# Two-layer decode with all gradients: gradient units taken out of the first attention's dp step, rows of g prepared one chunk sooner, two small output stores moved later

## Chip, cores and metric

The kernel runs on one core of one Trainium2 chip. The metric is the device time of one execution in microseconds (us), as the median of several runs. A core has TensorE (PE), which multiplies matrices into PSUM, VectorE (DVE), ScalarE (ACT) and GpSimd (POOL) for everything else, and SyncE (SP), which here only issues transfers. Transfers are also issued from the queues of ACT and POOL. All of them run on the same 16 DMA engines.

## The reference, cut to what matters

One token passes through attention A, a dense layer B, attention A again and B again. The same weights are used in both rounds. The output and the gradients of all inputs for a given `grad_out` are wanted.

```python
def _A_ref(x, k_cache, v_cache, wq, wo):            # Hq 32, Dh 128, Hkv 4, D 1024
    W = min(4096, max(256, Sk // 4))                # Sk 32768, so W = 4096
    q = (x @ wq) ...                                # one query row for each head
    k = jnp.repeat(k_cache[:, :, Sk - W:, :], rep, axis=1)
    v = jnp.repeat(v_cache[:, :, Sk - W:, :], rep, axis=1)
    p = _softmax(jnp.einsum("bhqd,bhkd->bhqk", q, k) * (Dh ** -0.5), axis=-1)
    return jnp.einsum("bhqk,bhkd->bhqd", p, v) ... @ wo

def _B_ref(x, w1, b1, w2):                          # F 3584
    h = jnp.einsum("bsd,df->bsf", x, w1) + b1
    act = h * jnp.tanh(softplus(h))
    return jnp.einsum("bsf,fd->bsd", act, w2)

x = A_x
x = x + _A_ref(_layernorm(x, axis=-1), A_k_cache, A_v_cache, A_wq, A_wo)
x = x + _B_ref(_layernorm(x, axis=-1), B_w1, B_b1, B_w2)
x = x + _A_ref(_layernorm(x, axis=-1), A_k_cache, A_v_cache, A_wq, A_wo)
x = x + _B_ref(_layernorm(x, axis=-1), B_w1, B_b1, B_w2)

_out, _vjp = jax.vjp(_f, A_x, A_k_cache, A_v_cache, A_wq, A_wo, B_w1, B_b1, B_w2)
_grads = _vjp(grad_out)
```

With one token, each weight is read for matrix-vector products, and each weight's gradient is a sum of two outer products, one for each round. The gradients of wq and wo are 8.4 MB each, those of w1 and w2 7.3 MB each. The gradients of the two caches are mostly zeros: 32768 rows for each of 4 heads, of which only the last 4096 take part.

## The kernel before

**Order.** The program is written by hand in the order in which each engine is to run it, and each engine works off its own queue in that order. It goes forward through A, B, A, B, then back: B of the second round (`dn_b1`), attention of the second round (`attn_bwd(1, ...)`), B of the first round, attention of the first round (`attn_bwd(0, ...)`), and a last stage that computes and stores the weights' gradients.

**Loads.** Weights come in chunks of 1 MB through a ring of eight slots (`ring`), which SP's queue fills in a planned order. The last loads are the eight chunks of wo for the first attention's backward (three of them in borrowed slots, which the program calls `lent`) and four chunks of wq; four more chunks of wq are still there from before.

**Zeros.** The zeros of the caches' gradients are 56 stores of 1 MB from the tile `zt`, issued by POOL (`zeros`, L265). The call can name a small tile, and POOL then first copies one element of it to `pz` (L260), so that the stores go out only when that tile is computed. In this way the zeros are spread over the run.

**First attention, backward** (`attn_bwd`, with l = 0). It goes in these steps; a hook is called in each, and the hooks of the first attention are `do1`, `dp1`, `dq1`, `dn1` and `units_a0`.
- *do*: eight chunks c of wo. Blocks are transposed on PE (L474), copied from PSUM to SBUF by ACT or DVE (`evac`, L306 and L309) and multiplied with the column of g (L493); some rows go to DVE (`rowdot`, L451). After each chunk comes `do1(c)`.
- *dp*: 128 small matmuls against V (L922) into two PSUM banks. For each bank DVE subtracts and multiplies, and the result goes to `DSX` (L928, L929). Then comes `dp1`.
- *dq*: 128 small matmuls of K with DSX (L938), then `DQC` (L940), its broadcast (L333) and `dq1`.
- *dn*: eight chunks t of wq, transposed and multiplied as in *do*. After each comes `dn1(t)`. The end is the layer norm's backward, with `units_a0` called twice inside, and the result is g0.

**Rows for the outer products.** A gradient unit (`unit_dw`, L1051) multiplies two rows of one operand with two rows of the other, one row for each round, so it wants these operands as rows on two partitions. They stand in `ROWS`, in four pairs of partitions that begin at 0, 32, 64 and 96. `rowize` transposes a set of columns on PE (L1010), lets ACT copy it to `rt` (L1013), and SP sends it into ROWS with two small DMAs (L1015). `rowize_f` does this with f's gradient through the tile `rf` (L857, L859, L861). `take_back` fetches rows that were put in DRAM earlier (L819). `twins` copies all pairs to a second set, `TWIN` (L1043), which units two blocks wide need. `store_rows` and `store_f` send the small outputs: `store_f` transposes b1's gradient `db` (L868), ACT copies it to the same `rf` (L870) and issues the store (L871); `store_rows` does so with `x4`, the output of the network, and with g0 (L321, L325, L326).

**Units.** `todo` holds four generators, one for each weight gradient. `work(n)` takes n steps from them in turn. A step makes 512 columns (PE, then `evac`) or, in the last stage, 1024; full stage tiles are stored by SP (L1025, or L1030 for a first half). `work` is called in `dp1` (four steps), in `units_a0` (twice four) and, until all is done, in the last stage. The stage tiles are K's and V's tiles as they come free, the ring's slots and the borrowed slots.

In *do*, chunk 5 has the hook that stores x4 and db, issues two zero stores and takes back four sets of rows; chunk 6 has `rowize` of `GA` and `GB` and `rowize_f`.

Of the kernel before, what the change touches and what calls it, by code (L numbers as in the profile page):

```python
# [23 lines left out]
TD = D // P  # L24
# [69 lines left out]
def kernel(  # L94
# [108 lines left out]
    GA = sb([P, TD, 2], BF16, "GA")  # L203
    GB = sb([P, TD, 2], BF16, "GB")
# [113 lines left out]
    def store_rows(col_bf, n, out_flat):  # L318

        b = big().bitcast(BF16)  # L320
        nc.tensor.transpose(b[0:n, 0:P], col_bf, ident_bf[:])  # L321
        k = so_n[0]
        so_n[0] += 1
        r = rt[0:n, 2 + k, :]
        nc.scalar.copy(r, b[0:n, 0:P])  # L325
        nc.scalar.dma_start(out_flat.rearrange("(t p) -> t p", p=P), r)  # L326
# [537 lines left out]
    def store_f(col):  # L864

        b = big().bitcast(BF16)
        for k in range(4):
            nc.tensor.transpose(b[0:7, k * P:(k + 1) * P], col[:].rearrange("p (c k) -> p k c", k=4)[:, k], ident_bf[:])  # L868
        r = rf[:, 0:512]
        nc.scalar.copy(r.rearrange("c (p k) -> c p k", k=4), b[0:7, 0:512].rearrange("c (k p) -> c p k", k=4))  # L870
        nc.scalar.dma_start(out_7.rearrange("(c j) -> c j", j=512), r)  # L871
# [135 lines left out]
    def rowize(cols, n, base, off):  # L1007

        b = big().bitcast(BF16)
        nc.tensor.transpose(b[0:2 * n, 0:P], cols[:].rearrange("p n l -> p (n l)"), ident_bf[:])  # L1010
        k = rt_n[0]
        rt_n[0] += 1
        nc.scalar.copy(rt[0:2 * n, k, :], b[0:2 * n, 0:P])  # L1013
        for l in range(2):
            nc.sync.dma_start(ROWS[base + l:base + l + 1, off:off + n * P].rearrange("o (t p) -> o t p", p=P),  # L1015
                              rt[l:2 * n:2, k, :])
# [96 lines left out]
    def work(n):  # L1113
        while n > 0 and any(todo):
            q = todo[turn[0] % 4]
            turn[0] += 1
            while q:
                try:
                    next(q[0])
                    n -= 1  # L1120
                    break
                except StopIteration:
                    q.popleft()
# [27 lines left out]
    x4 = sb([P, TD], BF16, "x4")  # L1151
    db = sb([P, TF], BF16, "db")
# [7 lines left out]
    def do1(c):  # L1160
        if c == 4:
            y = to_eight(YR, RT.rearrange("p a t s -> p (a t s)")[:, 0:512].bitcast(FP32))
            nc.vector.tensor_tensor(out=x4[:], in0=y, in1=x3[:], op=ALU.add)
        if c == 5:
            store_rows(x4[:], TD, out_0[0, 0, :])
            store_f(db)
            zeros(2, do1_acc[:, 4 * c:4 * c + 1])
        if c == 6:
            rowize(GA, TD, 32, 0)
            rowize(GB, TD, 96, 0)  # L1170
            rowize_f()
        if c == 5:
            take_back("AC", 96, NOFF)
            take_back("OC", 32, NOFF)
            take_back("NB", 64, 0)
            take_back("NA", 0, 0)

    def dp1():
        zeros(4)
        stage_free.extendleft(VS[:, g].rearrange("p t d -> p (t d)") for g in range(G))  # L1180
        work(4)

    def dq1():
        stage_free.extendleft(KT[:, g].rearrange("p t d -> p (t d)") for g in range(G))
# [4 lines left out]
    def dn1(t):  # L1189
        if t in (3, 6, 7):  # L1190
            zeros(2 if t == 3 else 1, dnp[:, t:t + 1])
        if t == 4:
            twins()
        if t == 5:
            todo[0].append(units_cols(0, 8, out_4))
# [8 lines left out]
    zeros(2, g0)  # L1204
    g0b = sb([P, TD], BF16, "g0b")
    nc.vector.tensor_copy(g0b[:], g0[:])
    store_rows(g0b[:], TD, out_1[0, 0, :])
    stage_free.extendleft(ring_t[:, i, :] for i in range(8))
    stage_free.extendleft(lent)
# [44 lines left out]
```

## Time and profile before

| | us |
|---|---|
| median of three runs | 458.82 (457.58 to 458.83) |
| profiled execution | 457.36 |
| its span, first to last instruction | 455.6 |
| PE busy | 317.9 (70%) |
| DVE busy | 261.9 (57%) |
| ACT busy | 210.6 (46%) |
| POOL busy | 38.9 (9%) |
| moved by DMA | 181.40 MB, mean 398 GB/s |

The span is that of one profiled execution; the execution's own time is 1.76 us longer. Busy shares are averages over stages with different limits. The windows of the profile list, for a stretch of the span, the busy time of each engine with the number of its instructions, then PE's granted clock, the busy share of the 16 DMA engines and their rate. The order of time lists start, length, engine, line, operation and shape; in brackets stands how long the engine was idle before, and what ended that. "SPq" and "POOLq" are the instructions of those engines that issue a transfer; when a transfer has landed is seen from who waited for it. The stages that the change touches are these: *do* of the first attention until 309.2 us, dp from 309.81, dq from 324.20, dn from 329.69, and the last stage from 349.48.

### The profile page before, as it was taken

What the parts mean: (1) busy time and instruction counts of PE and PEld (TensorE: products, weight loads), DVE (VectorE), ACT (ScalarE), POOL (GpSimd) and SP (SyncE); (2) the same over time, 40 slices, a digit from 0 to 9 for tenths busy, and PEclk for the clock granted to TensorE, in tenths of its full rate; (3) what the DMA queues carried; (4) which work ended last, traced back from release to release, by engine and by line L of the source; (5) the groups of instructions that cost most, each with busy time, mean ns of one, the idle gap of its engine ahead of it and who ended that gap; (6) DMA issues with size and microseconds to landing.
All of it is one profiled execution on the core that took longest, in us unless ns stands there. A gap on an engine that the chain in (4) does not pass through costs nothing. (4 is left out here: it accounts for less than half of the span.)

```text
span 455.6 us, 12833 instructions
## 1 busy us (share of the span) xinstructions
PE 317.9 (70%) x5681; PEld 244.5 (54%) x5681; DVE 261.9 (57%) x516; ACT 210.6 (46%) x244; POOL 38.9 (9%) x86
## 2 busy tenths in 40 slices
PE   3836443456798798986888577964696898789900
PEld 3835443445675698976887455954492122134500
DVE  4504737278532663763367558743176999988900
ACT  2501001011157675860373450750166999998900
POOL 1000000002032212102100001012112000000000
PEclk9955555565559897986698857995586555555555
DMA  8999999989999999999999999998399999999998
GB/s 335 419 423 420 416 420 420 418 316 422 391 426 420 423 421 414 400 420 422 425 416 423 424 393 365 422 418 359 129 368 404 412 410 420 415 422 419 404 409 324
DMA packets 28086, 181.40 MB, mean 398 GB/s; under 512 B 3675, under 2 KB 3703, under 8 KB 9591
## 3 DMA queue, kind: packets, MB, share of 16 engines
q1 hardware_dynamic: 19874, 121.84, 65.4%
q0 software_dynamic: 8064, 58.72, 31.3%
q8 instruction: 44, 0.72, 0.6%
q14 instruction: 12, 0.09, 0.0%
q10 hardware_dynamic: 92, 0.02, 0.0%
HBM read 81.84 MB, written 98.62 MB: 396 GB/s over the span
## 5 line engine op out<-in xcount | busy, mean ns | idle before, releaser
L309 ACT COPY ring<-BIG 128x1024 bf16<-128x1024 bf16 x51 | 50.6, 1013 | 49.7 <-PE BIG L474 44.5
L474 PE MATMUL BIG<-ident_bf,ring 128*128 128x128 bf16 x664 | 56.3, 242 | 4.4 <-ACT W L859 3.6
L474 PEld LDWEIGHTS <-ring 128*128 128x128 bf16 x768 | 54.6, 111 | 5.6 <-issue 5.1
L1051 PE MATMUL wide<-W 2*128 2x512 bf16 x228 | 50.3, 598 | 9.5 <-DVE KT L306 1.7
L451 DVE CUSTOM_DVE_ANT_0 junk<-ring,SC 128x1024 bf16<-128x1024 bf16 x32 | 38.9, 1215 | 9.2 <-DMA ring<-in_B_w_dram 8.8
L1051 PEld LDWEIGHTS <-W 2*128 2x128 bf16 x240 | 12.3, 102 | 53.6 <-issue 52.4
L493 PEld LDWEIGHTS <-ring 128*128 128x128 bf16 x864 | 30.1, 98 | 12.4 <-issue 6.1
L306 DVE COPY ring<-BIG 128x1024 bf16<-128x1024 bf16 x32 | 21.7, 689 | 25.1 <-PE BIG L474 14.0
L309 ACT CAST ring<-wide 128x1024 bf16<-128x1024 f32 (+1 forms) x36 | 33.8, 1028 | 2.3 <-PE wide L1051 1.3
L306 DVE CAST ring<-wide 128x1024 bf16<-128x1024 f32 (+1 forms) x28 | 32.6, 1199 | 3.1 <-PE wide L1102 1.0
L265 POOL DMA_DIRECT2D out_dram<-zt x56 | 29.7, 534 | 39.7 <-DMA out_dram<-zt 38.6
L309 ACT COPY KT<-BIG 128x1024 bf16<-128x1024 bf16 x22 | 21.7, 1008 | 22.4 <-PE BIG L652 20.5
L451 DVE CUSTOM_DVE_ANT_0 junk<-ring,DSX 128x1024 bf16<-128x1024 bf16 x24 | 29.4, 1224 | 0.8
L536 PE MATMUL MV<-NA,ring 128*128 128x1 bf16 x512 | 15.2, 165 | 13.0 <-DMA ring<-in_A_wq_dram 11.7
L474 PE MATMUL BIG<-ident_bf,W 128*128 128x128 bf16 x288 | 23.5, 228 | 0.4 <-issue 0.3
L309 ACT COPY W<-BIG 128x1024 bf16<-128x1024 bf16 x21 | 20.7, 1014 | 6.4 <-PE BIG L474 5.8
L306 DVE CAST KT<-wide 128x1024 bf16<-128x1024 f32 (+1 forms) x17 | 20.1, 1188 | 3.8 <-PE wide L1051 2.8
L536 PEld LDWEIGHTS <-ring 128*128 128x128 bf16 x512 | 14.6, 103 | 13.9 <-DMA ring<-in_A_wq_dram 12.4
L1102 PE MATMUL wide<-W 32*128 32x256 bf16 x128 | 21.0, 402 | 0.9 <-ACT ring L309 0.5
L309 ACT CAST VS<-wide 128x1024 bf16<-128x1024 f32 (+1 forms) x20 | 19.4, 1010 | 1.1 <-PE wide L1051 0.6
L474 PEld LDWEIGHTS <-W 128*128 128x128 bf16 x288 | 18.5, 112 | 0.7 <-issue 0.4
L347 PE MATMUL YR<-ring,AC 128*32 128x256 bf16 x208 | 10.3, 352 | 10.4 <-DMA ring<-in_B_w_dram 8.0
(272 smaller groups left out, 525.0 us busy)
## 6 DMA issues: line engine op xcount, KB each, us to landing
out_dram<-zt POOLq DMA_DIRECT2D x56, 1024.0 KB, 19.6
ring<-in_A_wq_dram SPq DMA_DIRECT2D x24, 1024.0 KB
ring<-in_A_wo_dram SPq DMA_DIRECT2D x14, 1024.0 KB
ring<-in_B_w_dram SPq DMA_DIRECT2D x13, 1024.0 KB
W<-in_A_wo_dram SPq DMA_DIRECT2D x10, 1024.0 KB
out_dram<-ring SPq DMA_DIRECT2D x8, 1024.0 KB
W<-in_B_w_dram SPq DMA_DIRECT2D x8, 896.0 KB
out_dram<-ring SPq DMA_DIRECT2D x11, 512.0 KB
```

The lines of the kernel that those rows point to most:

```text
L265: nc.gpsimd.dma_start(dst, zt[:])
L306: nc.vector.tensor_copy(dst, src)
L309: nc.scalar.copy(dst, src)
L347: nc.tensor.matmul(bank[32 * j:32 * j + 32, 0:n].rearrange("p (g a) -> p g a", a=m.shape[-1]), lhsT=vec.to_broadcast([P, 32]), rhs=m, star ...
L451: nc.vector.tensor_tensor_reduce(out=out, in0=a, in1=vec, scale=1.0, scalar=acc if i else 0.0, op0=ALU.mult, op1=ALU.add, accum_out=acc)
L474: nc.tensor.transpose(b[:, i * P:(i + 1) * P], block(w, i) if block else w[:, i * P:(i + 1) * P], ident_bf[:])
L493: nc.tensor.matmul(out, lhsT=w[:, i * P:(i + 1) * P], rhs=rhs_of(i), start=fresh[0], stop=last and i == n - 1, skip_group_check=True)
L536: nc.tensor.matmul(q_ps[:, h:h + 1], lhsT=ch[:, h * P:(h + 1) * P], rhs=NA[:, t, l:l + 1], start=(k == 0 and h == 0), stop=(k == TD - 1), ...
L1051: nc.tensor.matmul(b[:, 512 * i:512 * i + 512], lhsT=R[at:at + 2, lo:lo + P], rhs=R[at:at + 2, ro + 512 * i:ro + 512 * i + 512], start=Tru ...
L1102: nc.tensor.matmul(b[:, k * 256:(k + 1) * 256], lhsT=RT[32 * g:32 * g + 32, a, tp, :], rhs=YS[32 * g:32 * g + 32, :], start=True, stop=Tru ...
```

## The change

- `dp1` calls `work(4)` no more. The four units stay in `todo`.
- `rowize(GA)` and `rowize(GB)` come after chunk 5 instead of chunk 6. `rowize_f` stays after chunk 6.
- The four `take_back` calls come after chunk 6, behind `rowize_f`, instead of after chunk 5. On SP's queue the order is now GA and GB (four DMAs), f (two), AC, OC, NB, NA; it was AC, OC, NB, NA, GA and GB, f.
- `store_f(db)` moves from chunk 5 of *do* to chunk t = 1 of *dn*.
- `store_rows(x4)` moves from chunk 5 to the end of the attention's backward, ahead of `store_rows(g0b)`.

PE, DVE, POOL and SP have as many instructions as before. ACT has two fewer (243 for 245), because the four units that are left to the last stage are evacuated as two wide ones there.

```diff
@@ do1(c) @@
         if c == 5:
-            store_rows(x4[:], TD, out_0[0, 0, :])
-            store_f(db)
+            rowize(GA, TD, 32, 0)
+            rowize(GB, TD, 96, 0)
             zeros(2, do1_acc[:, 4 * c:4 * c + 1])
         if c == 6:
-            rowize(GA, TD, 32, 0)
-            rowize(GB, TD, 96, 0)
             rowize_f()
-        if c == 5:
             take_back("AC", 96, NOFF)
             take_back("OC", 32, NOFF)
             take_back("NB", 64, 0)
             take_back("NA", 0, 0)
@@ dp1() @@
         zeros(4)
         stage_free.extendleft(VS[:, g].rearrange("p t d -> p (t d)") for g in range(G))
-        work(4)
@@ dn1(t) @@
         if t in (3, 6, 7):
             zeros(2 if t == 3 else 1, dnp[:, t:t + 1])
+        if t == 1:
+            store_f(db)
         if t == 4:
             twins()
@@ after attn_bwd(0, ...) @@
     nc.vector.tensor_copy(g0b[:], g0[:])
+    store_rows(x4[:], TD, out_0[0, 0, :])
     store_rows(g0b[:], TD, out_1[0, 0, :])
```

## The prediction, made before the changed kernel ran

> **What bounds the kernel now.** I read the slices of the span first, then the windows of the last quarter, then the instructions in order of time around the one weak slice.
>
> ```profile
> DMA  8999999989999999999999999998399999999998
> GB/s 335 419 423 420 416 420 420 418 316 422 391 426 420 423 421 414 400 420 422 425 416 423 424 393 365 422 418 359 129 368 404 412 410 420 415 422 419 404 409 324
> ```
>
> A slice is 11.39 us. The DMA engines are full nearly everywhere; the slice at 319 to 330 moves 129 GB/s instead of some 415. The busy time by stretch says the same, finer:
>
> ```profile
> 305.00:350.00 45.00, 30.29 (x646) 25.10 (x646) 19.40 (x44) 15.25 (x22) 8.46 (x20) 0.63 0.78 314
> 308.00:310.00 2.00, 1.04 (x27) 0.90 (x28) 0.93 (x6) 0.00 (x0) 0.18 (x1) 0.50 0.76 303
> 310.00:312.00 2.00, 2.00 (x66) 2.00 (x64) 0.00 (x0) 0.00 (x0) 1.98 (x5) 0.50 0.59 230
> 320.00:322.00 2.00, 0.00 (x0) 0.00 (x0) 0.00 (x0) 0.00 (x0) 0.00 (x0) 0.50 0.72 293
> 322.00:324.00 2.00, 1.32 (x4) 0.16 (x4) 0.69 (x1) 0.95 (x2) 0.00 (x0) 0.50 0.05 20
> 326.00:328.00 2.00, 1.78 (x67) 1.69 (x64) 0.19 (x2) 0.00 (x0) 0.00 (x0) 0.50 0.00 0
> 328.00:330.00 2.00, 1.58 (x13) 1.30 (x14) 0.01 (x2) 0.26 (x1) 1.87 (x5) 0.50 0.34 131
> 340.00:342.00 2.00, 1.87 (x66) 1.68 (x62) 1.97 (x4) 0.30 (x1) 0.98 (x2) 1.00 0.72 270
> 350.00:433.00 83.00, 72.65 (x392) 25.79 (x384) 76.01 (x70) 78.95 (x86) 0.00 (x0) 0.50 1.01 414
> 433.80:452.00 18.20, 0.00 (x0) 0.00 (x0) 0.00 (x0) 0.00 (x0) 0.00 (x0) 0.50 1.02 408
> ```
>
> The last two columns are the DMA share and GB/s, the busy times before them PE, weight loads, VectorE (DVE), ScalarE (ACT), GpSimd (POOL). In the last row every engine is done and the DMA alone works for 18 us: the end is a queue of stores running dry, and the chain of waits, which calls ACT the bound up to 420 us, misses that. From 350 to 452 the share is 1.01 to 1.02 throughout. So the end falls earlier by just that DMA time which is idle before 350 and gets filled. Why it is idle stands in the order of time (column 1 start, column 2 length, in brackets the idle time before):
>
> ```profile
> 305.14 1.00 ACT L859 COPY W<-BIG 7x1024 bf16<-7x1024 bf16 x1 [4.05 <-DMA out_dram<-W]
> 306.20 0.81 PE L474 MATMUL BIG<-ident_bf,ring 128*128 128x128 bf16 x8 [3.57 <-ACT W L859]
> 310.06 2.10 POOL L265 DMA_DIRECT2D out_dram<-zt  x4
> 314.79 2.69 SPq L861 DMA_DIRECT2D W<-W  x2
> 322.43 1.01 PE L1051 MATMUL BIG<-W 2*128 2x512 bf16 x3 [8.55 <-DMA W<-W]
> 324.20 3.58 PE L938 MATMUL MV<-DSX,KT 128*128 128x8 bf16 x128
> 328.31 2.10 POOL L265 DMA_DIRECT2D out_dram<-zt  x4
> ```
>
> The four units of dp1 (L1051) wait at the head of PE's queue for rows of f that SP sent only at 314.79 to 317.48, and the dq matmuls (L938), which need none of them, stand behind. The next zero stores are tied to DQC, so the DMA engines run dry at 322. Earlier, rowize_f's copy (L859) waits for the store of b1's gradient to have left the shared row rf, PE waits for its bank, and the four zero stores of dp1 come late, at 310.06.
>
> **Change, part by part.**
> 1. *The store of db leaves c==5.* L859 waits for no store any more. PE's stall of 3.57 us goes; the ring copy that PE wanted next has its data (rowdot on that chunk ran at 300.47). dp1's zeros go from 310.06 to 306.5.
> 2. *No units in dp1.* The wait of 8.55 us and the units' own PE time (322.43 to 324.20, 1.77 us) go. With DSX's first half ready at 313.91 - 3.57 = 310.3 and its second at 311.8, the 3.58 us of dq run from 310.3 to 313.9, against 327.78: 3.57 + 8.55 + 1.77 = 13.9 us sooner. All that follows PE up to the last stage moves with it: the DQC zeros to 314.4, those at t = 3, 6, 7 (339.93, 344.60, 345.86) to 326.0, 330.7, 332.0, those on g0 (347.97) to 334.1, the first output store (351.16) to 337.3.
> 3. *The four units come back later:* units_a0 still makes eight, so four 512-column units are left to the last stage, where two are one evacuation of 1.01 us (ACT) or 1.22 us (DVE): about 1.1 us with the two engines side by side. The 18 us in which the DMA alone works cover it; without that cover it would cost 1.1.
> 4. *SP's order:* GA and GB rows (four DMAs) first, then f (two), then the four take-backs; ten small DMAs as before, behind the same loads. Six such issues took 10.58 us in a full queue (306.90 to 317.48), 1.76 each; ten from 297.3 end by 315. The DQC rows, ready at 329.67 - 13.9 = 315.8, are then not held. If the last six go out only from 311, when the loads are in, they end at 321.6: 6 us late for the twins, which the first wide stage unit (349.48 - 13.9 = 335.6) wants; in this trace the twins are issued by 337.78, 11.7 before it. I take nothing; the cover is the zeros, below.
> 5. *store_f in dn1 at t=1:* four transposes (0.38), a copy of 0.57 and an issue of 0.29 on ACT between ring copies with 0.6 to 0.7 us of idle each: nothing on the DMA's account. It waits for rowize_f's two DMAs to have read rf. Wanted at about 335.5 - 13.9 = 321.6; behind it on ACT stand all ring copies, for which PE waits. f's rows go out about 308 and, by the 5 us from 317.48 to 322.43, are in at 313. Nothing, with 8 us of room; the wait is rival four.
> 6. *x4's store before g0b's:* one transpose (0.22), one copy (0.26), one ACT issue (0.30), while PE and ACT wait for g0 anyway (1.32 us before L321): nothing; 0.8 at most.
>
> **Is the DMA then never dry?** One zero store is 1.05 MB, 2.56 us at 410 GB/s. From 306.5 to 323 the trace moved 338 GB/s x 16.5 us = 5.6 MB, all that was queued, dp1's four included; at 410 that lasts from 306.5 to 320.1. DQC's four (4.2 MB) come at 314.4 and last to 330.3; two at 326.0 to 335.4; two at 330.7 and 332.0 to 340.6; two at 334.1 to 345.7; outputs from 337.3. The margins are 5.7, 4.3, 4.7 and 8.4 us.
>
> **The sum.** Between 305 and 350 a share of 0.78 stands where 1.01 is full: 45 x (1.01 - 0.78)/1.01 = 10.2 us. By bytes: 314 x 45 = 14.1 MB takes 34.2 us at 414 GB/s (10.8 gained) or 35.3 at 400, about what zeros reached from 342 to 350 (9.7 gained). I take 10.2. Against it: the take-backs and rows that partly ran in a dip now run in full time. The take-backs are 38 KB in rows of 256 B, 152 of them; the small stores of the ACT queue between 296 and 332 used 0.1% of 16 engines' 36 us for 30 packets, 19 ns each, so 152 cost 2.9 us of one engine: 0.2 us if spread over 16, 2.9 if one engine carries all and everything ends with it. I take 0.4, near the spread end, since part ran under load before as well. Net 9.8: the span goes from 455.6 to 445.8, that execution from 457.36 to 447.6. The median of the runs shown, 458.82, lies 1.46 above the profiled execution; taken from it, **449.0**, which I forecast.
>
> **Rivals.**
> *Two engines carry the rows.* Each take-back ends on two partitions, so its rows may use two DMA engines, which then trail the rest by 2.9/2 = 1.45 us to the end. For it: 452 to 454 us shows a share of 0.62, so some engines do end later than others. Against: big stores follow on all engines and can only be late at the very end. Gain 10.2 - 1.45 = 8.75: 450.1. The Trainium skill (DMA: Bandwidth & Descriptors, "Why a DMA increments its semaphore by 16 and not by 1") says that a DMA runs on the largest number of engines up to 16 that divides the slowest dimension of both sides, which is two here; the trace does not name engines.
>
> *The first dip stays.* If ACT's copies, not the store's wait, pace the last wo chunk, dp starts no earlier and 2 x (1.01 - 0.76)/1.01 + 2 x (1.01 - 0.59)/1.01 = 1.3 us at 308 to 312 stay. dq is still 10.3 sooner, in time for the second dip. 458.82 - 8.5 = 450.3. For it: ACT has two ring copies (1.90 us) behind L859. Against: PE's stall names L859.
>
> *The dip moves.* The rows land late (point 4, behind zeros that now fill the DMA), and units_a0 (344.25 - 13.9 = 330.4) or the first wide stage waits. Outputs late by L leave a hole of L - 8.4. At L = 13, 4.6 us: 453.6. For it: 5 us from issue to use under load. Against: the rows are issued 15 us before their use. The Trainium skill (same page, "Queues, rings and completion order") says that an engine takes turns between queues by packets, so small rows would pass a long queue of zeros; the 5 us, under four queued zero stores (10 us of work), agree.
>
> *Slower: store_f holds ACT.* If f's rows are read late, ACT stops at t = 1, PE runs out of banks, and the zeros at t = 3 come late; beyond 4.3 us of hold the DMA runs dry, and beyond 4.3 + 9.8 = 14.1 us the kernel is slower than before, as when f is read at 336 instead of 313. At 16 us: 460.7. For it: this very row cost ACT 4.05 us in the other direction. Against: SP sends f sixth at the latest, and even sent from 311 on it is read at 326.6, a hold of 5 us that costs 0.7.
>
> *It does nothing:* if the end were set by engines (ACT 78.95 of 83 us busy), filling the DMA would bring nothing; but the engines, too, start 13.9 sooner, and they stop 18 us before the end. 458.8.
>
> **Chances.** Forecast 0.60 (449.0, its own range 447.4 to 450.0), two engines 0.12 (450.1), first dip stays 0.13 (450.3), dip moves 0.08 (451 to 456), does nothing 0.03, slower 0.04. The low end takes 10.8 by bytes and the spread of the runs (the lowest is 1.2 under the median): 446.7. The high end, 452.6, takes in the two middle rivals and the small part of the moved dip. What this measurement can tell from no change is about 0.3%, 1.4 us: faster 0.93, within it 0.03, slower 0.04.
>
> **What would show it.** Right: no ACT wait at L859; no L1051 between L922 and L938; dq over by about 314; the DQC zeros at 314 to 315; DMA share 1.0 in every slice from 305 on; the last unit some 10 to 14 us sooner than 433.76, the DMA alone for 15 us or more behind it. Wrong: a stretch under 0.9 between 320 and 350; ACT waiting at L870 for a DMA; PE waiting at L1051 for W<-W in units_a0 or the first wide units; last stores on a few engines only.

## The result, and the profile after

| | before | after |
|---|---|---|
| median (us) | 458.67 (457.58 to 458.83) | 450.82 (450.36 to 451.38) |
| ratio, 95% interval | | 0.9834 [0.9815, 0.9854] |
| span of the profiled execution (us) | 455.6 | 448.6 |
| last unit evacuated (us) | 433.76 | 423.05 |
| DMA mean (GB/s) | 398 | 404 |

The kernel is 7.85 us faster by the medians and 7.0 us by the two spans; the prediction said 9.8. The weak slice is gone, and a new weakness stands at the very end. These are the slices of the span after the change (11.2 us each; first row the DMA share in tenths, second what was moved):

```profile
DMA  8999999979999999999999999999999999999993
GB/s 336 420 420 418 421 420 418 418 312 427 393 421 422 422 420 415 398 420 423 424 423 422 427 423 419 424 393 422 424 406 415 400 417 419 417 421 408 377 408 143
```

The slice of 129 GB/s has become one of some 400. The last slice, 324 before, is 143 now. The windows of the kernel after say both more finely; the last two columns are DMA share and GB/s, the ones before them busy times of PE, weight loads, DVE, ACT and POOL and PE's clock:

```profile
305.00:350.00 45.00, 35.78 (x615) 24.27 (x613) 26.47 (x45) 22.81 (x31) 7.49 (x18) 0.62 1.01 416
308.00:310.00 2.00, 0.85 (x27) 0.78 (x27) 1.41 (x3) 0.00 (x0) 0.00 (x0) 0.50 1.00 415
...
322.00:324.00 2.00, 2.00 (x57) 2.00 (x54) 1.35 (x4) 1.75 (x2) 0.00 (x0) 1.00 1.04 436
...
326.00:328.00 2.00, 1.50 (x54) 1.44 (x55) 1.97 (x4) 0.01 (x1) 0.45 (x1) 1.00 1.02 395
...
430.00:440.00 10.00, 0.00 (x0) 0.00 (x0) 0.00 (x0) 0.00 (x0) 0.00 (x0) 0.50 1.02 407
440.00:444.00 4.00, 0.00 (x0) 0.00 (x0) 0.00 (x0) 0.00 (x0) 0.00 (x0) 0.50 0.28 114
444.00:446.00 2.00, 0.00 (x0) 0.00 (x0) 0.00 (x0) 0.00 (x0) 0.00 (x0) 0.50 0.06 27
446.00:448.60 2.60, 0.00 (x0) 0.00 (x0) 0.00 (x0) 0.00 (x0) 0.00 (x0) 0.50 0.03 13
```

Between 305 and 350 the share went from 0.78 to 1.01; both dips, at 308 and at 322 to 330, are filled. But from about 441 on almost nothing moves, and the span still lasts until 448.6. A share of 0.06 is one sixteenth: one DMA engine of 16 works, at 27 GB/s, which is a sixteenth of the 407 to 415 that all move together. Fifteen engines are out of work some 7 us before the end, and one is not; its last packet starts at 447.28. (The 1.3 us after that move nothing; the kernel before has 1.2 us of this kind.) Before the change the last stretch was far shorter: share 1.02 until 452, 0.62 in the next 2 us, 0.02 in the last 1.6.

The order of time after the change, for the places at which the prediction looked (start, length, engine, line, operation; in brackets the idle time before and what ended it):

```profile
299.38 1.00 ACT L859 COPY W<-BIG 7x1024 bf16<-7x1024 bf16 x1
...
304.24 2.10 POOL L265 DMA_DIRECT2D out_dram<-zt  x4
...
309.80 3.05 PE L938 MATMUL MV<-DSX,KT 128*128 128x8 bf16 x109 [1.08 <-issue]
...
313.38 2.10 POOL L265 DMA_DIRECT2D out_dram<-zt  x4
...
321.26 0.57 ACT L870 COPY W<-SC 7x512 bf16<-7x512 bf16 x1 [0.18 <-PE SC L868]
...
328.03 4.98 SPq L1043 DMA_DIRECT2D W<-W  x4
...
338.63 1.04 PE L1051 MATMUL wide<-W 2*128 2x512 bf16 x7 [1.72 <-DMA W<-W]
```

rowize_f's copy (L859) has no wait in brackets any more. dp's four zero stores leave at 304.24 instead of 310.06. No unit stands between dp and dq; the dq matmuls are over at 312.85 instead of 327.78, and DQC's zeros leave at 313.38 instead of 328.31. The last line is a wait that was not there before: the first wide units waited 1.72 us for the twins, whose four DMAs SP issued from 328.03 to 333.01.

**Where the time went, by idle DMA time.** Because the bytes are the same (181.40 MB), the span is the time in which the DMA is full plus the time in which it is not. I count the idle time of a stretch as its length times (1.01 - share)/1.01. From 305 to 360 (share 0.83 before, 1.01 after) it was 55 x 0.18/1.01 = 9.8 us and is 0. In the last stretch it was (2 x 0.39 + 1.6 x 0.99)/1.01 = 2.3 us and is (4 x 0.73 + 2 x 0.95 + 2.6 x 0.98)/1.01 = 7.3 us. So 9.8 us were gained and 5.0 us given back, together 4.8 of the 7.0. Most of the rest lies before the change acts: from 260 to 305 the profiled execution of before moved 399 GB/s and that of after 415, 0.72 MB or 1.7 us. That is not the change's doing: a kernel in which nothing ahead of 305 is altered (the first experiment) has 415 there as well, and the profiled executions of all twelve experiments have 407 to 422. A dip of 0.8 us at 419 to 423 in the changed kernel (share 0.70 and 0.90) is not in this sum.

### The profile page after: what moved, and what is told of

Its sections match the earlier page's. It is cut to its first block, busy times and chain, and to the rows that moved or that the text cites. A ratio compares the mean times of both kernels' runs of the same rounds, so it can differ in the third digit from the quotient of the medians.

```text
span 448.6 us, 12825 instructions
## 1 busy us (share of the span) xinstructions
PE 313.9 (70%) x5681; PEld 239.7 (53%) x5681; DVE 261.2 (58%) x516; ACT 210.0 (47%) x242; POOL 38.9 (9%) x86
## 2 busy tenths in 40 slices
DMA packets 28085, 181.40 MB, mean 404 GB/s; under 512 B 3674, under 2 KB 3702, under 8 KB 9590
## 4 chain that ended last, share of the span: by engine, by line
DMA 53%; PE 22%; ACT 7%; DVE 7%; issue 4%; SPq 1%; ACTq 0%; DVEq 0%
DMA ring<-in_B_w_dram 13%; DMA W<-in_A_wo_dram 8%; PE BIG L474 8%; DMA ring<-in_A_wq_dram 7%; DMA ring<-in_A_wo_dram 5%; DMA W<-in_A_wq_dram 5%; ACT ring L309 4%; DMA out_dram<-W 4%; DMA W<-in_B_w_dram 4%; PE TP L493 3%; DMA W<-dr_AC 2%; DMA W<-in_A_k_cache_dram 2%; PE wide L1051 2%; DVE KT L306 2%; PE SC L347 2%
## 5 line engine op out<-in xcount | busy, mean ns | idle before, releaser
L309 ACT COPY ring<-BIG 128x1024 bf16<-128x1024 bf16 x52 | 51.5, 1014 | 49.3 <-PE BIG L474 45.0
L1051 PE MATMUL wide<-W 2*128 2x512 bf16 x232 | 51.7, 597 | 10.7 <-ACT ring L309 1.7
L474 PE MATMUL BIG<-ident_bf,ring 128*128 128x128 bf16 x672 | 54.3, 233 | 1.8 <-issue 1.0
L474 PEld LDWEIGHTS <-ring 128*128 128x128 bf16 x768 | 52.0, 108 | 3.4 <-issue 2.6
L451 DVE CUSTOM_DVE_ANT_0 junk<-ring,SC 128x1024 bf16<-128x1024 bf16 x32 | 38.9, 1215 | 11.6 <-DMA ring<-in_B_w_dram 11.2
L1051 PEld LDWEIGHTS <-W 2*128 2x128 bf16 x240 | 12.6, 102 | 48.1 <-issue 43.7
L493 PEld LDWEIGHTS <-ring 128*128 128x128 bf16 x864 | 29.9, 98 | 10.0 <-issue 5.8
L309 ACT CAST ring<-wide 128x1024 bf16<-128x1024 f32 x35 | 33.9, 1040 | 2.0 <-PE wide L1051 0.9
L306 DVE COPY ring<-BIG 128x1024 bf16<-128x1024 bf16 x32 | 21.8, 689 | 12.8 <-PE BIG L474 10.2
L536 PEld LDWEIGHTS <-ring 128*128 128x128 bf16 x512 | 14.7, 104 | 14.0 <-DMA ring<-in_A_wq_dram 12.5
L1102 PE MATMUL wide<-W 32*128 32x256 bf16 x128 | 20.0, 403 | 0.9 <-ACT ring L309 0.6
L309 ACT CAST KT<-wide 128x1024 bf16<-128x1024 f32 x18 | 17.7, 1064 | 3.2 <-PE wide L1051 3.0
L306 DVE CAST KT<-wide 128x1024 bf16<-128x1024 f32 (+1 forms) x14 | 15.4, 1141 | 6.3 <-PE wide L1051 6.2
```

The lines of the kernel that those rows point to most:

```text
L306: nc.vector.tensor_copy(dst, src)
L309: nc.scalar.copy(dst, src)
L451: nc.vector.tensor_tensor_reduce(out=out, in0=a, in1=vec, scale=1.0, scalar=acc if i else 0.0, op0=ALU.mult, op1=ALU.add, accum_out=acc)
L474: nc.tensor.transpose(b[:, i * P:(i + 1) * P], block(w, i) if block else w[:, i * P:(i + 1) * P], ident_bf[:])
L493: nc.tensor.matmul(out, lhsT=w[:, i * P:(i + 1) * P], rhs=rhs_of(i), start=fresh[0], stop=last and i == n - 1, skip_group_check=True)
L536: nc.tensor.matmul(q_ps[:, h:h + 1], lhsT=ch[:, h * P:(h + 1) * P], rhs=NA[:, t, l:l + 1], start=(k == 0 and h == 0), stop=(k == TD - 1), ...
```

## The experiments

After the result two questions were open. Which part of the change brings the gain? And what makes one engine end some 6 us behind the others: the small rows, as a rival had it, or something that was there before and that the gap had hidden?

**1. The units alone.** The kernel before, without the call in dp1:

```diff
     stage_free.extendleft(VS[:, g].rearrange("p t d -> p (t d)") for g in range(G))
-    work(4)
```

> The kernel before with only the four units taken out of dp1. Theory A (the end is the DMA queue running dry, so what counts is filled DMA time): the PE wait of 8.55 us and 1.77 us of units go, the dip from 320 to 330 is filled, the dip at 308 to 312 (1.3 us) stays because rowize_f still waits for db's store; some 1.3 us less gain than the whole change, about 452 us. Theory B (the wait on db's store and the order of the rows carry much of the gain): 455 us or more. Both expect the share in the last 8 us to show whether one DMA engine trails.

Measured: 450.62 us (450.25 to 451.37), ratio 0.9845 [0.9827, 0.9863] to before. That is the whole gain of the change, and better than theory A's 452; the other four edits add nothing that can be measured. Its order of time shows what it lacks:

```profile
302.67 1.00 ACT L859 COPY W<-BIG 7x1024 bf16<-7x1024 bf16 x1 [2.53 <-DMA out_dram<-W]
...
311.49 3.56 PE L938 MATMUL MV<-DSX,KT 128*128 128x8 bf16 x128
```

L859 still waits for the store of db, 2.53 us here, and dq ends at 315.05 instead of 312.85. Of the dip that was expected at 308 to 312 some 0.5 us are left (share 0.92 and 0.87 from 306 to 310, 1.00 from 305 to 360), and they cost nothing that the time shows. Its end has the lone engine, too (share 0.18, 0.09 and 0.04 in the three stretches of 2 us from 442 on).

**2. The moves alone.** All of the change, but dp1 keeps `work(4)`:

```diff
         stage_free.extendleft(VS[:, g].rearrange("p t d -> p (t d)") for g in range(G))
+        work(4)
```

> The whole change, but the four units stay in dp1. If the earlier issue of f's rows brings them in before dp ends, the PE wait at L1051 is gone and the time is 451 to 452 us. If small rows queue behind the zero stores (in the changed kernel f's rows, issued at 301.34 to 307.16, land late), PE still waits 8 us or more at L1051, the dip between 320 and 330 comes back and the time is 456 to 458 us.

Measured: 456.43 us (455.86 to 456.57), ratio 0.9966 [0.9953, 0.9979] to before. SP's rows of f and PE's wait for them, in its order of time:

```profile
302.13 5.84 SPq L861 DMA_DIRECT2D W<-W  x2
...
321.02 1.00 PE L1051 MATMUL BIG<-W 2*128 2x512 bf16 x3 [11.63 <-DMA W<-W]
```

The rows were issued from 302.13 to 307.97 instead of 314.79 to 317.48, 9.5 to 12.7 us sooner, and PE got them only 1.4 us sooner, at 321.02 instead of 322.43. The landing events of the trace, of which each of these DMAs leaves one for each of its seven rows (besides one right after the issue), tell what PE waited for: six rows of the second DMA had landed by 313.05, the seventh landed at 320.89, 7.8 us later. In the kernel before, all seven landed between 321.80 and 322.30. So the early rows waited for one late landing, as the end does. As long as the units stood in dp1, the moves could do little.

**3. Rows sent one by one.** If take-backs and twins with their two partitions load two engines, spreading them should shorten the tail:

```diff
-        nc.sync.dma_start(ROWS[base:base + 2, ...], r)
+        for l in range(2):
+            nc.sync.dma_start(ROWS[base + l:base + l + 1, ...], r[l:l + 1])
...
-            nc.sync.dma_start(TWIN[base ^ 32:(base ^ 32) + 2, 0:n], ROWS[base:base + 2, 0:n])
+            for l in range(2):
+                nc.sync.dma_start(TWIN[...].rearrange("o (a b) -> o a b", a=16),
+                                  ROWS[...].rearrange("o (a b) -> o a b", a=16))
```

> The changed kernel with each take-back and each twin sent row by row, a twin row in 16 pieces, so that no two DMA engines carry them. In the profile of the changed kernel one DMA engine works alone from 441.5 to 447.5 us. Theory rows (the two-partition DMAs put 2.8 us on two engines, which then trail): the lone stretch shrinks by 2.8 us or more, 447.5 to 448.5 us. Theory other (the lag has another origin): the lone stretch stays at 5 to 6 us, 450.8 +- 0.6.

Measured: 451.42 us (450.92 to 451.62), ratio 0.9857 [0.9842, 0.9872] to before. The tail is short (share 1.04 until 446, then 0.47 for 2 us, then 0.02). But the eight issues of the twins lasted from 331.18 to 340.77, units waited for them, and two new dips opened. Two windows of this kernel:

```profile
338.00:340.00 2.00, 1.74 (x6) 0.55 (x6) 1.01 (x5) 1.75 (x5) 0.47 (x2) 0.50 0.29 109
...
346.00:348.00 2.00, 1.53 (x9) 0.21 (x6) 1.11 (x1) 1.61 (x2) 0.00 (x0) 0.50 0.09 34
```

By itself this tells nothing of the rows, because two things changed at once. It gave the better idea, though: a gap and a short tail come together, as in the kernel before.

**4. Two engines loaded on purpose.** Three more copies, each of two partitions, to a scratch in DRAM, issued in dn:

```diff
+            for i in range(3):
+                nc.sync.dma_start(extra[i][:], VS[2 * i:2 * i + 2].rearrange("p g t d -> p (g t d)"))
```

> The changed kernel with three more copies of two partitions of V (64 KB each, 196 KB in all) to a scratch in DRAM behind the twins; it computes the same. If the bytes alone counted, 196 KB at 410 GB/s are 0.5 us: 451.3. If two-partition DMAs run on two engines (three times 32 KB each at 27 GB/s is 3.6 us) and the trailing engine is one of them: 454.4, with a lone stretch of some 10 us. If they run on two engines but another one trails: 450.8 and a lone stretch no longer than before.

Measured: 452.53 us (452.24 to 453.05), ratio 0.9884 [0.9869, 0.9899] to before, 1.7 us more than the changed kernel. Its last windows:

```profile
442.00:444.00 2.00, 0.00 (x0) 0.00 (x0) 0.00 (x0) 0.00 (x0) 0.00 (x0) 0.50 0.21 86
...
446.00:448.00 2.00, 0.00 (x0) 0.00 (x0) 0.00 (x0) 0.00 (x0) 0.00 (x0) 0.50 0.18 72
```

Now 0.18 x 16 = 3 engines work to the end instead of one. The time is none of the three that were expected. The three last landings of the last store come 5.5, 6.0 and 7.1 us behind the median of its 16, in the changed kernel 0.3, 0.7 and 6.4. So the transfers of two rows made two more engines late, and they stay late until the end; the one that was late already is hardly later than before. It does not say that the rows of the kernel are what made the one late.

**5. A gap on purpose.** The changed kernel, but DQC's four zero stores wait until dn's t = 2:

```diff
 def dq1(): ...
-        zeros(4, DQC[:, 0, 0:1])
 def dn1(t): ...
+        if t == 2:
+            zeros(4, dnp[:, t:t + 1])
```

> The changed kernel with the four zero stores of dq1 issued only after chunk t = 2 of dn (about 322.8 us instead of 313.4), so that the DMA engines run dry from about 319 to 323. Theory catch-up (one DMA engine is some 3 us behind when the loads end, a gap lets it catch up, without one it trails to the end): the gap costs the fifteen others time that they would spend idle at the end anyway; the time stays at 450.8 to 451.8 and the lone stretch at the end shrinks from 6 us to 3 or less. Theory sum (each us of idle DMA costs a us): 454 to 455 us, and the lone stretch stays.

Measured: 453.63 us (452.77 to 455.38), ratio 0.9908 [0.9879, 0.9938] to before, 2.9 us above the changed kernel (450.73 in run 7). The catch-up theory had at most 451.8 and the sum theory 454 to 455, for a gap of some 4 us; it came out longer. Windows of the gap and of the end:

```profile
318.00:320.00 2.00, 2.00 (x22) 2.00 (x21) 0.69 (x1) 1.30 (x2) 0.00 (x0) 0.50 0.13 52
320.00:322.00 2.00, 2.00 (x37) 2.00 (x36) 1.38 (x2) 0.74 (x2) 0.00 (x0) 0.76 0.13 39
322.00:324.00 2.00, 2.00 (x54) 1.87 (x52) 1.83 (x3) 1.40 (x3) 0.00 (x0) 1.00 0.15 42
...
446.00:448.00 2.00, 0.00 (x0) 0.00 (x0) 0.00 (x0) 0.00 (x0) 0.00 (x0) 0.50 0.84 338
448.00:450.00 2.00, 0.00 (x0) 0.00 (x0) 0.00 (x0) 0.00 (x0) 0.00 (x0) 0.50 0.12 49
```

In the gap the share is not 0 but 0.13 to 0.15, two engines' worth, which fits late engines that work on while the others are dry. The idle time from 305 to 360 is 55 x 0.13/1.01 = 7.1 us, the span only 2.7 us longer, and the idle time at the end is 3.4 us instead of 7.3. So 3.9 us of the gap were paid back at the end.

**6. No rows at all.** The changed kernel without the four take-backs and without the twins, so that the units read what stands there; that part of the output is not computed:

```diff
-            take_back("AC", 96, NOFF)
-            take_back("OC", 32, NOFF)
-            take_back("NB", 64, 0)
-            take_back("NA", 0, 0)
...
-        if t == 4:
-            twins()
```

> The changed kernel without the four take-backs and without the twins: those rows are left as they were, so that the gradients of the weights are not the reference's; units, stores and waits for the other rows stay. Theory rows (take-backs and twins put 2.8 us on two engines, one of which trails): the lone stretch at the end falls from 6 to 3 us, the time to 447.5 to 448.5. Theory other (the lag is there without them): lone stretch of 5 us or more, 450 to 451 us.

Measured: 450.81 us (450.12 to 451.07), ratio 0.9839 [0.9816, 0.9863] to before. Two of its last windows:

```profile
442.00:444.00 2.00, 0.00 (x0) 0.00 (x0) 0.00 (x0) 0.00 (x0) 0.00 (x0) 0.50 0.07 29
444.00:446.00 2.00, 0.00 (x0) 0.00 (x0) 0.00 (x0) 0.00 (x0) 0.00 (x0) 0.50 0.06 27
```

The same lone engine, with the same lag. Take-backs and twins are not its cause.

**7. The changed kernel again**, beside runs 5 and 6, with no edit:

> The changed kernel once more, beside the others on the same chip: 450.8 +- 0.6. If the lone stretch belongs to the kernel and not to one execution, a second profile shows it again with 5 to 7 us; if it is chance, it differs by more than 2 us.

Measured: 450.73 us (450.26 to 451.03), ratio 0.9839 [0.982, 0.9858] to before. Its tail has 0.07, 0.07 and 0.04 from 442 to 448: the late engine is no accident of one execution.

**8 and 9. The last megabyte on one half of the engines.** The second of g0's zero stores is sent in a shape of eight rows, 15/16 of the bytes first and then 1/16 (run 8), or in the other order (run 9):

```diff
-    zeros(2, g0)
+    zeros(1, g0)
+    last = zjobs.pop().rearrange("(a b) c -> a b c", a=8)
+    for part in (slice(1, 16), slice(0, 1)):
+        d8 = last[:, part]
+        nc.gpsimd.dma_start(d8, zt[0:8, None, :].to_broadcast([8, d8.shape[1], ZC]))
```

> The changed kernel, but the very last 1 MB zero store (1.05 MB, the second of the two tied to g0) is sent as two stores of eight rows instead of one of 128 partitions: 15/16 of the bytes first, then 1/16. The same bytes, the same time of issue; only how the bytes are dealt out to DMA engines should differ. Theory (one DMA engine trails and alone sets the end: share 0.06 to 0.07 at 27 GB/s over the last 6 us): a store of eight rows would use eight of the 16 engines, so each of eight gets 131 KB (5.0 us at 26 GB/s) instead of 66 KB (2.5 us), and the other eight get nothing. If the trailing engine is among the eight, the end is about 2.5 us later: 453.2; if it is among the others, 2.5 us sooner: 448.2. This kernel and the next one should lie on opposite sides of 450.8, some 4 to 5 us apart. Rival (the end is set by bytes, or by the order in which stores finish, not by one engine): both within 0.6 of 450.8. Second rival (a store of eight rows is not dealt out to half of the engines): both about equal, both later or both unchanged. The Trainium skill (DMA: Bandwidth & Descriptors, "Why a DMA increments its semaphore by 16 and not by 1") states that a transfer from GpSimd whose slowest dimension allows only k engines goes to k consecutive ones from a cursor that moves on; by it the two kernels take the two halves.

> As the kernel before it, with the two stores of eight rows in the other order: 1/16 of the bytes first, then 15/16. Theory (one trailing engine): if the two stores go to one half of the engines and then to the other, the large part now goes to the other half, so this kernel ends on the other side of 450.8 than its twin: 448.2 where that gives 453.2, or 453.2 where that gives 448.2. In the faster of the two the lone tail (share 0.06 to 0.07) is some 2.5 us shorter or hidden behind the eight engines that carry the last store, in the slower one it is longer. Rival (bytes alone): both within 0.6 of 450.8. Second rival (not dealt out by halves): equal to its twin.

Measured: 465.52 us (464.3 to 467.0), ratio 1.0163 [1.0132, 1.0194] to before, and 464.88 us (462.05 to 466.41), 1.0147 [1.0109, 1.0184]. Both are some 14 us slower than the changed kernel, which neither theory nor rival had. The DMA issues of run 8 (KB of each, and us from issue to landing) and its first output stores:

```profile
out_dram<-zt POOLq DMA_DIRECT2D x55, 1024.0 KB, 20.7
...
out_dram<-zt POOLq DMA_DIRECT2D x1, 960.0 KB, 31.0
```

```profile
341.90 17.46 SPq L1030 DMA_DIRECT2D out_dram<-KT  x4
```

The store out of eight partitions landed after 31.0 us (20.7 is the median of the others, most of it time in a queue), and SP took 17.46 us for four output stores that it issues in 4.17 in the changed kernel. The slices of run 8 fall to 266, 107 and 237 GB/s between 337 and 372. So this edit tested something else: one slow transfer out of few partitions that holds up all that shares its engines. It decides nothing on the late engine. Whether the few partitions or the rows read over and over from them make it slow is not separated.

**10. A smaller gap.** Two of DQC's four zero stores wait until t = 2:

```diff
-        zeros(4, DQC[:, 0, 0:1])
+        zeros(2, DQC[:, 0, 0:1])
...
+        if t == 2:
+            zeros(2, dnp[:, t:t + 1])
```

> The changed kernel with two of the four zero stores of dq1 moved to dn's t = 2. The kernel with all four moved there had 7.4 us in which the DMA engines were dry before t = 2; two stores fill 5.1 us of them (2.56 us each), so some 2.3 us of a gap stay, between about 323 and 326. Theory (a gap costs nothing until the trailing engine has caught up, because that engine works on through it): no change, 450.8 within 0.6, and a lone tail (share 0.06 to 0.07) that is shorter than the 6 us of the changed kernel by about the gap, some 4 us. Rival (idle time of all engines counts one for one, as in the prediction's sum): 453.1, and the lone tail as before.

Measured: 450.98 us (450.44 to 452.29), ratio 0.984 [0.9824, 0.9855] to before. This is the theory's figure, but the gap came out smaller than reckoned. Its widest window:

```profile
322.00:324.00 2.00, 2.00 (x57) 2.00 (x54) 1.35 (x3) 1.58 (x3) 1.09 (x3) 1.00 0.62 232
```

With the windows beside it (0.97, 0.94, 0.99) that is 1.0 us of idle time, not 2.3. The rival would then have had 451.7, which the interval (450.3 to 451.8 on 458.42) still holds. The tail didn't shrink by 4 us either: the last landing of the last store is 6.2 us behind the median, 6.4 in the changed kernel. Weak evidence for the theory.

**11. A probe for the late engine.** Seven tiny stores behind the last store on SP's queue, of sizes that nothing else has:

```diff
     work(10000)
+    for k in (1, 2, 3, 4, 6, 8, 12):
+        probe = dram.tile([k, 16 + 8 * k], BF16, name=f"probe_{k}")
+        nc.sync.dma_start(probe[:], ident_bf[0:k, 0:16 + 8 * k])
```

> The changed kernel with seven tiny stores behind the last store on SP's queue, to a scratch in DRAM: 1, 2, 3, 4, 6, 8 and 12 rows of 48, 64, 80, 96, 128, 160 and 224 bytes. Sizes that nothing else has, so the packets of each can be told apart in the record of packets. One engine trails by some 6 us at the end; a packet on it must wait for its backlog, and the others go at once. If one engine is always the same, all tiny stores that reach it have their last packet at the very end, and the ones that do not reach it are over sooner. The Trainium skill (DMA: Bandwidth & Descriptors, "Why a DMA increments its semaphore by 16 and not by 1") states that such a store from SP goes to the lowest-numbered engines, as many as it has rows here: by it, the smallest store with a late packet names the engine: 1 row: engine 0, 2 rows: engine 1, 12 rows: one of 8 to 11, none: one of 12 to 15. Theory: exactly one packet of each store from some number of rows on is late, by up to 6 us. Rival (several engines end late by turns, or the tail is one long transfer and no engine's backlog): no packet late, or several of one store. Time: 450.8, at most 1 us more for the issues behind the last store.

Measured: 451.57 us in its one run. The start of each packet of these sizes, from the trace's record of packets, in us from the span's start:

```
rows  bytes  packets
1     48     442.75
2     64     441.84 442.76
3     80     442.78 442.78 442.79
4     96     444.02 444.03 444.05 444.08
6     128    445.29 445.30 445.30 445.31 445.34 447.81
8     160    446.51 446.52 446.52 446.52 446.54 446.55 446.57 447.82
12    224    447.77 to 447.88, all twelve
```

Of the store of two rows one packet goes 0.9 us behind the other, together with that of the store of one row; those of three and four rows have no late packet. The store of six rows has exactly one, 2.5 us behind its fellows, and so has that of eight, 1.3 us behind; both go at 447.8, when the end is reached. The store of twelve went out too late to tell. So a packet on one certain engine waits for that engine's backlog, and stores of up to four rows don't meet it (the engine that delayed the first two stores was free from 442.75 on). The Trainium skill (DMA: Bandwidth & Descriptors, "Why a DMA increments its semaphore by 16 and not by 1") states that a store from SP goes to the lowest-numbered engines; the one late packet of the stores of six and eight rows, and none in those of three and four, agrees with a fixed order, and by it the engine is the fifth or the sixth.

**12. Less for the late engine.** Three quarters of the columns of the last zero store leave in 125 partitions and 3, from SP's queue:

```diff
-    zeros(2, g0)
+    zeros(1, g0)
+    last = zjobs.pop()
+    for rows, cols in ((slice(125, 128), slice(0, 3072)), (slice(0, 125), slice(0, 3072)), (slice(0, 128), slice(3072, ZC))):
+        nc.sync.dma_start(last[rows, cols], zt[rows, cols])
```

> In the probe the stores of 6 and 8 rows had one late packet each, those of 1 to 4 rows none: one engine of the fifth and sixth trails. Here three quarters of the columns of the last 1 MB zero store leave from SP's queue in 125 partitions (983 KB x 3/4 x 1.05 = 0.77 MB) and 3 partitions; the rest of it goes as usual, in 128. Nothing else changes. Theory: the 0.77 MB go to five engines, 154 KB each instead of 48 KB, and the trailing engine is not among them: it gets 48 KB less, at 27 GB/s 1.8 us, and the five get 106 KB, 3.9 us, more, which still leaves them 2 us or more ahead of it. Time 449.0 (1.8 less than 450.8), and a tail on some six engines until 2 us before the end, then on one. Rival 1 (the trailing engine is one of the five, or changes from run to run): 454.7, or a wide spread between the two. Rival 2 (bytes alone, or the 0.77 MB still go to all engines): 450.8 within 0.6. The Trainium skill (DMA: Bandwidth & Descriptors, "Why a DMA increments its semaphore by 16 and not by 1") states that a transfer goes to the largest number of engines up to 16 that divides its slowest dimension, the lowest-numbered ones where SP issues it; 125 gives five by it.

Measured: 455.78 us (454.7 to 456.33), ratio 0.9946 [0.9932, 0.996] to before: 5.0 us slower than the changed kernel. Two of its windows:

```profile
350.00:355.00 5.00, 4.87 (x22) 1.07 (x20) 4.93 (x6) 5.00 (x7) 0.00 (x0) 0.50 0.79 303
...
448.00:450.00 2.00, 0.00 (x0) 0.00 (x0) 0.00 (x0) 0.00 (x0) 0.00 (x0) 0.50 0.21 86
```

From 446 on some five engines work (share 0.34), from 448 some three (0.21), from 450 one (0.07). The time is close to the first rival's 454.7 (the late engine is one of the five). But the profile explains most of the 5 us otherwise: the first output store left at 344.11 instead of 340.31, 3.3 us of DMA time are idle between 305 and 360, and two slices ahead of the edit move 390 and 391 GB/s where the changed kernel has 393 and 422. So the time alone is inconclusive. The landings say more: of the store issued at 350.55, eleven come within 0.6 us of the median and five 4.4 to 8.2 us behind it. Had the late engine not been among the five that carried the 0.77 MB, six would be late; so it is one of them, as the first rival had it, and by the order of the probe it is the fifth. None of the twelve runs is faster than the changed kernel beyond the intervals.

**What the runs say together.** The idle DMA time of each profiled execution, by the shares of its windows as above, in us (the shares have two digits, so the middle column is good to about 0.5; the end holds some 1.2 us behind the last packet in each):

| kernel | span | idle, 305 to 360 | idle at the end | rest |
|---|---|---|---|---|
| before | 455.6 | 9.8 | 2.3 | 443.5 |
| 2, moves only | 454.7 | 9.3 | 3.4 | 442.0 |
| 5, gap on purpose | 451.3 | 7.1 | 3.4 | 440.8 |
| 3, rows spread | 449.8 | 5.4 | 2.8 | 441.6 |
| 4, two engines loaded | 450.6 | 1.1 | 7.5 | 442.0 |
| 6, no rows | 448.9 | 1.1 | 6.9 | 440.9 |
| 10, small gap | 449.1 | 0.5 | 6.8 | 441.8 |
| 11, probe | 449.8 | 0.5 | 7.9 | 441.4 |
| 12, less for one | 454.0 | 3.3 | 6.8 | 443.9 |
| 1, units only | 448.7 | 0.5 | 6.5 | 441.7 |
| 7, changed again | 448.5 | 0 | 7.3 | 441.2 |
| changed | 448.6 | 0 | 7.3 | 441.3 |

Runs 8 and 9 are left out. The rest is nearly constant, 441 to 442 for most; before and run 12 have some 2 us more, of which the 1.7 us of before lie ahead of the change. Four kernels have 5 us or more of idle time in the middle, and all of these end with 2.3 to 3.4 us of it; seven have 1.1 us or less, and end with 6.5 to 7.9; run 12 lies between and doesn't follow. So about 4 us of idle time in the middle cost nothing, and what is longer costs about one for one: the changed kernel and run 5 differ by 7.1 us in the middle, 3.9 at the end and 2.7 in span.

The mechanism is an engine that is late before the gap, works through it and so catches up. The trace shows this directly. Each store of 128 partitions leaves 16 landing events, and the last of them belongs to the lone engine: in the changed kernel its last five groups of packets end at 442.29, 443.54, 444.78, 446.03 and 447.28, and the last landings of the last five stores follow 0.40 to 0.47 us behind these. That it is the same engine all along is inferred, since the events don't name it. The table tells by how many us the last landing of a store comes behind the median of its 16. Where there is a long gap, it lies between the second column and the third (in run 5 the four stores of the third are those of t = 2):

| kernel | dp's four zero stores | DQC's four zero stores | last output store |
|---|---|---|---|
| 2, moves only (gap) | 5.4 to 6.1 | 1.5 to 2.7 | 2.2 |
| 5, gap on purpose (gap) | 5.0 to 7.8 | 1.5 to 2.4 | 2.3 |
| before (dip, then gap) | 2.3 to 2.5 | 1.2 to 2.1 | 1.2 |
| changed | 5.5 to 7.1 | 7.0 to 7.6 | 6.4 |
| 7, changed again | 4.9 to 7.0 | 6.9 to 7.6 | 6.4 |
| 1, units only | 4.7 to 4.9 | 5.0 to 5.2 | 5.8 |
| 6, no rows | 5.3 to 5.9 | 6.0 to 6.6 | 6.1 |

In the kernel before, the first dip, at 308 to 312, comes ahead of dp's zero stores; the loads ahead of it were up to 7.9 us late. The lag is much older than the change: in the kernel before, the zero store issued at 166.93 has 3.8 us of it, that of 172.49 has 7.9 and that of 207.92 has 8.0. A gap of 5 us or more brings it down to 1 to 3 us, and without one it stays until the end. Why the engine falls behind is not shown: only that take-backs and twins are not the cause.

## Why the prediction was right, point by point

**What bounds the kernel: right.** The end is a queue of stores that runs dry, and idle DMA time ahead of it is what can be gained. Engines end their work at 423 in the changed kernel, 25 us before the span ends, and nothing shows there but DMA.

**Step 1, the store of db: right in its mechanism, worth nothing.** L859 has no wait and dp's zeros left at 304.24, earlier than the 306.5 reckoned (1.3 us of this lie ahead of the change: POOL's copy for chunk 5's zeros ran at 295.68 instead of 296.95). Experiment 1, in which the wait stays, is as fast as the whole change, which fits that a dip shorter than the late engine's lag is free.

**Step 2, no units in dp1: right, and all of the gain.** dq was over at 312.85 (314 in the prediction), DQC's zeros left at 313.38 (314.4), those at t = 3, 6 and 7 at 325.39, 330.13 and 331.40 (326.0, 330.7, 332.0), those of g0 at 334.21 (334.1). The first output store left at 340.31 (337.3): 3.0 us late, of which the wait for the twins is 1.72.

**Step 3, units at the end: right.** The last unit ended 10.7 us sooner, not 13.9, and was covered by 25 us of DMA.

**Step 4, SP's order: off, without a price.** Ten small issues were to end by 315 or, at worst, by 321.6. The take-backs left between 316.92 and 320.75, and DQC's rows stood behind them until 320.86. The twins kept PE waiting for 1.72 us. The zeros of g0 covered that, as the step had said: the DMA share from 335 to 350 is 1.01. Experiment 2 shows what the step did not reckon with: a small DMA is complete when its latest row is, and one of seven rows landed 7.8 us behind the others.

**Steps 5 and 6: right in the outcome, step 5 by luck.** ACT's copy of db (L870, at 321.26) waited 0.18 us, for PE and not for a DMA. But f's rows were not in at 313: all but one of each DMA had landed by 312.94, the last at 320.78. Of the 8 us of room 0.5 were left. x4's store sits in the wait for g0.

**The margins: right.** Read in windows of 2 us, the share between 305 and 349 is nowhere under 0.97.

**The sum: here it failed.** The term of 10.2 for the filled gap was right in size (9.8 by shares to 360). The term beside it, "0.4 for the small rows", was the only one for what the end could lose, and the end lost 5.0. The error is in the sentence "So the end falls earlier by just that DMA time which is idle before 350 and gets filled": a mean share of 1.01 was read as 16 engines that end together. One was late from before 190 us on, and the gap had absorbed that lag. The rival *two engines* saw that some engine could trail to the end, and its figure, 450.1, is nearer than the forecast; but its cause, the take-backs on two partitions, fell with experiment 6, and the trailing is one engine for some 6 us, not two for 1.45. By the sum the span was to end at 445.8, and it ended at 448.6. These 2.8 us are less than the 5.0 lost at the end in part because 1.7 us were gained from 260 to 305, where the profiled execution of before was slow; the medians differ by 1.8 (450.82 for 449.0). That much of the nearness is luck.

**The signs of being wrong.** Two of the four came: last stores on a few engines only, and PE waiting at L1051 for W<-W at the first wide units (1.72 us). The first was the one that mattered.

**The other rivals.** *First dip stays* and *dip moves* fell with the windows from 305 to 350; *it does nothing* and *store_f holds ACT* fell with the time and with L870.

## What to carry to other kernels

Where a kernel ends on a DMA queue that runs dry, don't price an idle stretch of the DMA engines at its full length: an engine that lags uses it to catch up, and only what exceeds its lag is gained (here 4 to 5 us of 10 were free). The end of the kernel before does not show the lag, because its gap has removed it; the spread of the 16 landings of a store ahead of the gap does (8.0 us for the zero store of 207.92). At the end of a kernel without a gap it shows as a share of one or two sixteenths. Work that waits for a transfer must not stand at the head of an in-order queue ahead of work that feeds the DMA: taking four units out of dq's way was the whole gain, and sending their rows sooner, with the units left there, brought 1.6 us. A large store out of eight partitions cost the kernel some 14 us, because the stores beside it waited.

## What the runs showed of the hardware

- One of 16 DMA engines ended some 6 us after the others in both profiled executions of the changed kernel and in the one without take-backs and twins (share 0.05 to 0.07, 20 to 29 GB/s; last landing 6.1 to 6.4 us behind the median). In the probe it was one certain engine's packets that were late. The cause is open.
- An idle stretch let that engine catch up: its lag fell from 6.1 to 1.6 us over the gap of run 2 and from 7.8 to 1.8 over that of run 5.
- A store of 983 KB out of eight partitions took 31.0 us from issue to landing and slowed other stores (107 GB/s for a whole slice, four output stores issued in 17.46 us instead of 4.17), while the stores out of 128 partitions at the end of the changed kernel keep 407 GB/s.
- A small DMA can be held by one late engine: of the seven rows of f that were issued until 307.97 in run 2, six had landed by 313.05 and the seventh at 320.89, which ended an 11.63 us wait of PE.
- A store out of 125 partitions left five landing events, besides one right after the issue (run 12); stores of 128 partitions leave 16.
